# A cached-attention decode block: V as the moving operand, wo in three parts, c and x as rows

## The chip, the core and the metric

The kernel runs on one core of a Trainium2 chip. Such a core has five engines that run side by side[...]: TensorE (PE, matrix products, whose weight loads are shown as PEld), VectorE (DVE), ScalarE (ACT), GpSimd (POOL) and SyncE (SP, which here only issues transfers). Sixteen DMA engines move data between memory (HBM) and the on-chip buffer (SBUF); matrix products land in a small accumulator memory (PSUM). The metric is the time of one execution on the device in microseconds (us). Before the change it is 360.23 us, the median of 3 runs (360.12 to 360.32).

## What is computed

One token goes through a transformer block with modulation (adaLN): a modulation vector from `c`, a layer norm, attention over a cache of 32768 positions with 32 query heads on 8 kv heads of 128, an output projection, and a ReLU feed-forward of 1792. Everything is bf16 in memory.

```python
mod = (_silu(c) @ w_mod).reshape(c.shape[0], 6, 1, -1)
sa, ca, ga, sb, cb, gb = (mod[:, i] for i in range(6))
h = _layernorm(x) * (1 + ca) + sa
q = (h @ wq).reshape(B, Sq, 32, 128).transpose(0, 2, 1, 3)
scores = einsum('bhqd,bhkd->bhqk', q, repeat(k_cache, 4)) * 128 ** -0.5
o = einsum('bhqk,bhkd->bhqd', softmax(scores), repeat(v_cache, 4))
x = x + ga * (o.transpose(0, 2, 1, 3).reshape(B, Sq, 4096) @ wo)
h = _layernorm(x) * (1 + cb) + sb
x = x + gb * (maximum(h @ w1, 0) @ w2)
```

The K cache and the V cache hold 64 MB each; with the weights (w_mod 3 MB, wq 4, wo 4, w1 1.75, w2 1.75) some 149 MB have to be read for one token.

## The kernel before

**The stream.** All large inputs come through one ring of eight SBUF slots (`ring`, L71), in the order of the list `stream` (L114 to L123), by transfers that SP issues one after the other (`load`, L110). A transfer is issued when its slot is free, that is, when what was in the slot has been used. `need(key)` makes the list advance up to that key. The order is: two parts of w_mod, two of wq, four K tiles of head 0, then for each kv head g the K tiles of head g+1 and the V tiles of head g in turn; the first half of wo ahead of the last head's V tiles, then the second half of wo, w1 and three parts of w2 (1, 0.5 and 0.25 MB). A K or V tile is 2 MB: 128 partitions by 64 positions by 128. A head has four of each (NTILE = 4).

**The start.** `c` and `x` are loaded by the ACT queue with 4 elements to a partition (L134, L135), and cast (L174, L176). From c come the SiLU (L212 to L218) and 96 matmuls for the modulation (L226); `rows4` (L233) turns a column vector into four rows; `layernorm_T` (L181) does the norm with a matmul for the sums (L189); 128 matmuls give the queries (L267). POOL clears the buffers `qbd` and builds identities.

**One head.** `scores(g, u)` (L296) transposes a K tile in two halves on DVE (L309) and does 16 matmuls of 512 columns with the block-diagonal queries `qbd` as weights (L318). `softmax(g)` (L329) finds the maximum through two small matmuls (L334, L346), does the exponent on ACT (L351), transposes the probabilities on DVE (`PT_g`, L356) and gets the sums by a matmul (L361). `pv(g, u)` (L366) multiplies V: each of the 64 blocks of 128 positions is loaded as weights and met by four columns of PT_g, so that a tile costs 64 weight loads and 64 matmuls of four columns (L374), with the result transposed already. `normalise(g)` (L379) divides by the sums and spreads the result over `oA` with a mask `cmask`; `spread(b)` (L392) makes from four heads the operand `o2` for the projection; `project(b)` (L402) does 64 matmuls against half of wo (L407). The loop (L414 to L433) interleaves scores of head g+1 with pv of head g. The first half of wo is projected ahead of the last head's V tiles, the second after them.

**The tail.** With the attention summed in `attnT_ps`, DVE forms x1T (L438, L439), `layernorm_T` gives h2T, 56 matmuls the hidden vector (L450), ACT the ReLU (L455); `rows4` turns x1T into rows (L456), then 56 matmuls of 128 columns multiply by w2 (L465) as its parts land; two DVE operations (L471, L473) scale and add, and SP issues the output (L474).

[...] The transfers of the ring carry an order token, so that SP keeps their order; the rest is ordered by dependences and priorities (`tc.high_priority()` around L324).

Of the kernel before, what the change touches and what calls it, by code (L numbers as in the profile page):

```python
# [9 lines left out]
BF16 = mybir.dt.bfloat16  # L10
# [7 lines left out]
def kernel(  # L18
# [14 lines left out]
    nc = tc.nc  # L33
# [11 lines left out]
    NG = NTILE // 2  # L45
    GH = 4
    HH = GH * REP
    CH = P // HH
    RH = Dh // CH
    NHALF = Hkv // GH  # L50
    FB = 2
# [11 lines left out]
    wq_v = A_wq.rearrange("(p kt) n -> p kt n", p=P)  # L63
    wo_v = A_wo.rearrange("(b p r) d -> b p r d", p=P, r=RH)
    w1_v = B_w1.rearrange("(p kt) f -> p kt f", p=P)
# [20 lines left out]
    def load(key):  # L86
        kind = key[0]
        if kind == "wm":
            t = ring.tile([P, KT // 2, 6 * D], BF16, tag="slot", name="wm_sb")
            src = wm_v[:, 2 * key[1]:2 * key[1] + 2, :]  # L90
        elif kind == "wq":
            t = ring.tile([P, KT // 2, Hq * Dh], BF16, tag="slot", name="wq_sb")
            src = wq_v[:, 2 * key[1]:2 * key[1] + 2, :]
        elif kind == "k":
            t = ring.tile([P, TK, Dh], BF16, tag="slot", name="Ksb")
            src = kv[key[1], key[2]]
        elif kind == "v":
            t = ring.tile([P, TK, Dh], BF16, tag="slot", name="Vsb")
            src = vv[key[1], key[2]]
        elif kind == "wo":  # L100
            t = ring.tile([P, RH, D], BF16, tag="slot", name="wo_sb")
            src = wo_v[key[1]]
        elif kind == "w1":
            t = ring.tile([P, KT, Dff], BF16, tag="slot", name="w1_sb")
            src = w1_v
        else:
            a0, n = W2P[key[1]]
            t = ring.tile([P, n, FB, D], BF16, tag="slot", name="w2_sb")
            src = w2_v[:, a0:a0 + n]
        i = nc.sync.dma_start(out=t[:], in_=src)  # L110
        tc.stamp_issue_order_token(i.ins, "sp_stream")
        loaded[key] = t

    stream = [("wm", 0), ("wm", 1), ("wq", 0), ("wq", 1)]  # L114
    stream += [("k", 0, u) for u in range(NTILE)]
    for g in range(Hkv):
        if g == Hkv - 1:
            stream.append(("wo", 0))
        for u in range(NTILE):
            if g + 1 < Hkv:  # L120
                stream.append(("k", g + 1, u))
            stream.append(("v", g, u))
    stream += [("wo", 1), ("w1",)] + [("w2", i) for i in range(len(W2P))]  # L123
    pos = [0]
# [7 lines left out]

    xc_bf = const.tile([P, 2, KT], BF16)
    nc.scalar.dma_start(out=xc_bf[:, 0, :], in_=c[0].rearrange("(p kt) -> p kt", p=P))  # L134
    nc.scalar.dma_start(out=xc_bf[:, 1, :], in_=A_x[0, 0].rearrange("(p kt) -> p kt", p=P))  # L135

# [10 lines left out]
    for hp in range(4):  # L147
# [11 lines left out]

    cmask = const.tile([P, CH], F32)  # L160
    nc.vector.tensor_reduce(
        out=cmask[:], in_=ident_f[:].rearrange("p (c r) -> p c r", r=RH), op=ALU.add, axis=AX.X,
    )
    rsel_f = const.tile([P, RH], F32)
    nc.vector.tensor_reduce(
        out=rsel_f[:], in_=ident_f[:].rearrange("p (c r) -> p r c", r=RH), op=ALU.add, axis=AX.X,
    )
    rsel = const.tile([P, RH], BF16)
    nc.vector.tensor_copy(out=rsel[:], in_=rsel_f[:])
    oT_sb = const.tile([P, Hq], BF16)  # L170
    oA = [const.tile([P, HH, CH], BF16, name=f"oA{i}") for i in range(NHALF)]

    cT = const.tile([P, KT], F32)
    nc.vector.tensor_copy(out=cT[:], in_=xc_bf[:, 0, :])  # L174
    xT = const.tile([P, KT], F32)
    nc.vector.tensor_copy(out=xT[:], in_=xc_bf[:, 1, :])  # L176

# [3 lines left out]
    def layernorm_T(src_T, stat_in, dst_T, shiftT, nscaleT, tagp):  # L181
# [6 lines left out]
        stat_ps = small_ps([P, 2], f"stat_ps_{tagp}")  # L188
        nc.tensor.matmul(stat_ps[:], lhsT=onesD_f[:], rhs=stat_in[:], start=True, stop=True)  # L189
        nu = const.tile([P, KT], F32, name=f"nu_{tagp}")  # L190
# [21 lines left out]
    e_t = const.tile([P, KT], F32)  # L212
    nc.scalar.activation(out=e_t[:], in_=cT[:], func=ACT.Exp, scale=-1.0)
    nc.vector.tensor_scalar(out=e_t[:], in0=e_t[:], scalar1=1.0, scalar2=None, op0=ALU.add)
    sig = const.tile([P, KT], F32)
    nc.vector.reciprocal(out=sig[:], in_=e_t[:])
    siluT = const.tile([P, KT], BF16)
    nc.vector.tensor_tensor(out=siluT[:], in0=cT[:], in1=sig[:], op=ALU.mult)  # L218

# [12 lines left out]

    def rows4(src_T, name):  # L233

        r_ps = small_ps([P, P], f"{name}_ps")
        nc.vector.memset(r_ps[:], 0.0)
        for i in range(KT):
            dst = r_ps[32 * i:32 * i + 1, :].rearrange("o (n kt) -> o kt n", kt=KT)
            for kt in range(KT):
                nc.tensor.matmul(  # L240
                    dst[:, kt, :], lhsT=src_T[:, kt:kt + 1], rhs=ident_f[:, 32 * i:32 * i + 32],
                    start=True, stop=True, skip_group_check=True,
                )
        r_sb = const.tile([P, P], F32, name=f"{name}_sb")
        nc.vector.tensor_copy(out=r_sb[:], in_=r_ps[:])
        return r_sb

    gb_rows = rows4(modT_sb[:, 5 * KT:6 * KT], "gb_rows")

    hT = const.tile([P, KT], BF16)  # L250
    stat1 = const.tile([P, 2], F32)
    nc.vector.reduce_sum(out=stat1[:, 0:1], in_=xT[:], axis=AX.X)
    nca = const.tile([P, KT], F32)
# [6 lines left out]
    )  # L260
    layernorm_T(xT[:], stat1, hT[:], modT_sb[:, 0:KT], nca[:], "ln1")

# [103 lines left out]
    def pv(g, u):  # L366
        if u == 0:
            o_tiles[g] = ps_o.tile([P, REP], F32, tag="o", name="oT_ps")
        oT_ps, PT_g = o_tiles[g], PT_tiles[g]
        Vsb = need(("v", g, u))  # L370
        G, s0 = u // 2, 4 * (u % 2)
        for j in range(TK):
            c0 = (16 * G + j % 16) * 32 + REP * (s0 + j // 16)
            nc.tensor.matmul(  # L374
                oT_ps[:], lhsT=Vsb[:, j, :], rhs=PT_g[:, c0:c0 + REP],
                start=(u == 0 and j == 0), stop=(u == NTILE - 1 and j == TK - 1),
            )

    def normalise(g):  # L379

        b, gl = divmod(g, GH)
        o_g = oT_sb[:, REP * g:REP * (g + 1)]
        nc.vector.tensor_tensor(out=o_g, in0=o_tiles.pop(g)[:], in1=Linv_tiles.pop(g)[:], op=ALU.mult)  # L383
        nc.vector.tensor_tensor(
            out=oA[b][:, REP * gl:REP * (gl + 1), :],
            in0=o_g.unsqueeze(2).to_broadcast([P, REP, CH]),
            in1=cmask[:].unsqueeze(1).to_broadcast([P, REP, CH]), op=ALU.mult,
        )

    o2_tiles = {}  # L390

    def spread(b):  # L392

        o2_ps = small_ps([P, RH], "o2_ps")
        nc.tensor.matmul(
            o2_ps[:], lhsT=oA[b][:].rearrange("p h c -> p (h c)"), rhs=rsel[:], start=True, stop=True,
        )
        o2 = spool.tile([P, RH], BF16, tag="o2_sb", name="o2_sb")
        nc.vector.tensor_copy(out=o2[:], in_=o2_ps[:])
        o2_tiles[b] = o2  # L400

    def project(b):  # L402
        o2 = o2_tiles.pop(b)
        wo_sb = need(("wo", b))
        for r in range(RH):
            for ko in range(KT):
                nc.tensor.matmul(  # L407
                    attnT_ps[:, ko:ko + 1],
                    lhsT=wo_sb[:, r, :].rearrange("p (m ko) -> p ko m", ko=KT)[:, ko, :],
                    rhs=o2[:, r:r + 1], start=False, stop=(b == NHALF - 1 and r == RH - 1),  # L410
                    skip_group_check=True,
# [6 lines left out]
    for g in range(Hkv):  # L418
        if g + 1 < Hkv:
            build_qbd(g + 1)  # L420
        for u in range(NTILE):
            if g + 1 < Hkv:
                scores(g + 1, u)
            pv(g, u)
        PT_tiles.pop(g)
        if g + 1 < Hkv:
            softmax(g + 1)
        normalise(g)
        if g % GH == GH - 1:
            spread(g // GH)  # L430
        if g == Hkv - 2:
            project(0)
    project(1)  # L433


    stat2 = const.tile([P, 2], F32)
    x1T = const.tile([P, KT], F32)
    nc.vector.tensor_tensor(out=x1T[:], in0=attnT_ps[:], in1=modT_sb[:, 2 * KT:3 * KT], op=ALU.mult)  # L438
    nc.vector.scalar_tensor_tensor(  # L439
        out=x1T[:], in0=x1T[:], scalar=1.0, in1=xT[:], op0=ALU.mult, op1=ALU.add, accum_out=stat2[:, 0:1],  # L440
    )
    h2T = const.tile([P, KT], BF16)
    layernorm_T(x1T[:], stat2, h2T[:], modT_sb[:, 3 * KT:4 * KT], ncb[:], "ln2")

    w1_sb = need(("w1",))
# [9 lines left out]
    nc.scalar.activation(out=hidT[:], in_=hidT_ps[:], func=ACT.Relu)  # L455
    x1_rows = rows4(x1T[:], "x1_rows")  # L456
    ffn_ps = small_ps([P, P], "ffn_ps")
    nc.vector.memset(ffn_ps[:], 0.0)
    for part, (base, n) in enumerate(W2P):
# [10 lines left out]
    o_rows = const.tile([P, P], F32)  # L470
    nc.vector.tensor_tensor(out=o_rows[:], in0=ffn_ps[:], in1=gb_rows[:], op=ALU.mult)  # L471
    o_bf = const.tile([P, P], BF16)
    nc.vector.tensor_tensor(out=o_bf[:], in0=o_rows[:], in1=x1_rows[:], op=ALU.add)  # L473
    nc.sync.dma_start(  # L474
        out=out[0, 0].rearrange("(i n) -> i n", i=KT),
# [32 lines left out]
```

## Time and profile before

| | us or share |
|---|---|
| median of 3 runs | 360.23 us |
| the profiled execution's own time | 360.0 us |
| its span, first to last instruction | 358.2 us |
| PE busy (matmuls) | 237.5 us, 66% |
| PE weight loads | 136.9 us, 38% |
| DVE busy | 184.5 us, 52% |
| ACT busy | 27.0 us, 8% |
| mean granted PE clock | 0.77 |
| HBM read | 149.42 MB, 417 GB/s over the span |

The span is what the profile sees; the execution's own time is 1.8 us longer. A row of the profile names the line, the engine, the operation, the tile written and those read, and how often; busy time of an engine that waits for something else costs nothing. These groups are touched by the change (busy us and mean ns of one, then idle time before them and what ended it):

```
L318 PE MATMUL S_ps<-KTt,qbd 128*128 128x512 bf16 x512 | 159.1, 475 | 59.8 <-DVE KTt L309 58.9
L374 PE MATMUL oT_ps<-PT_g,Vsb 128*128 128x4 bf16 x2048 | 56.6, 164 | 9.5 <-DMA Vsb<-in_A_v_cache_dram 5.1
L407 PE MATMUL attnT_ps<-o_sb,wo_sb 128*128 128x1 bf16 x128 | 4.6, 172 | 2.3 <-DMA wo_sb<-in_A_wo_dram 2.3
L174 DVE CAST cT<-xc_bf 128x4 f32<-128x4 bf16 x1 | 3.8, 3764 | 4.2 <-DMA xc_bf<-in_c_dram 4.2
```

Matmuls are pipelined, so the mean of one (475 ns) is longer than the step from one to the next. The small loads of c and x land 4.4 and 8.5 us after their issue; a K or V tile lands 34 us after its issue, since it stands behind those issued before it.

### The profile page before, as it was taken

How to read it: one execution, taken by the hardware profiler on the slowest of the kernel's cores; microseconds unless marked ns; L12 is line 12 of the kernel's file. 1: busy time of each engine (PE TensorE's matmuls, PEld its weight loads, DVE VectorE, ACT ScalarE, POOL GpSimd, SP SyncE). 2: the span in 40 equal slices, each digit the busy share in tenths (PEclk: the TensorE clock that was granted, in tenths of full speed). 3: DMA queues.
4: the chain of work that ended last, by engine and by line, in shares of the span. 5: the costliest groups of instructions: out<-in, count | busy, mean ns of one | idle time of the engine just before them, and what ended most of it. 6: DMA issues, size and time to landing. Idle time of an engine off the chain costs nothing.

```text
span 358.2 us, 6817 instructions
## 1 busy us (share of the span) xinstructions
PE 237.5 (66%) x3138; PEld 136.9 (38%) x3138; DVE 184.5 (52%) x207; ACT 27.0 (8%) x65; POOL 8.3 (2%) x13
## 2 busy tenths in 40 slices
PE   0547775857587839755777758883956576895454
PEld 0543333433254425423343425341523334445354
DVE  4419976552954465553954385456655394342012
ACT  1111022002000110002000200011000100003000
POOL 9000000000000000000000000000000000000000
PEclk9999996986597659876698659686968869665555
DMA  7999999999999999999999999999999999999993
GB/s 302 428 434 423 430 437 432 417 435 432 434 421 437 428 426 432 434 424 432 434 429 424 432 429 435 426 426 432 428 435 427 423 435 434 426 426 435 426 413 119
DMA packets 11492, 149.86 MB, mean 418 GB/s; under 512 B 1480, under 2 KB 1480, under 8 KB 2376
## 3 DMA queue, kind: packets, MB, share of 16 engines
q1 hardware_dynamic: 11176, 149.43, 98.0%
q8 instruction: 24, 0.39, 0.4%
q10 hardware_dynamic: 288, 0.00, 0.0%
q14 instruction: 4, 0.03, 0.0%
HBM read 149.42 MB, written 0.00 MB: 417 GB/s over the span
## 4 chain that ended last, share of the span: by engine, by line
DMA 77%; DVE 11%; PE 10%; issue 1%; ACT 0%; DVEq 0%
DMA Ksb<-in_A_k_cache_dram 67%; DVE KTt L309 9%; DMA wo_sb<-in_A_wo_dram 9%; PE S_ps L318 6%; PE oT_ps L374 1%; DMA xc_bf<-in_c_dram 1%; PE attnT_ps L407 1%; PE ffn_ps L465 0%; PE hidT_ps L450 0%; ACT P_g L351 0%; DVE PT_g L356 0%; PE x_rows_ps L240 0%; DVE S_g L324 0%; PE stat_ps_ln L189 0%; PE L_ps L361 0%
## 5 line engine op out<-in xcount | busy, mean ns | idle before, releaser
L318 PE MATMUL S_ps<-KTt,qbd 128*128 128x512 bf16 x512 | 159.1, 475 | 59.8 <-DVE KTt L309 58.9
L309 DVE STREAM_TRANSPOSE KTt<-Ksb 128x2048 f32<-128x2048 f32 x64 | 143.7, 2286 | 47.6 <-DMA Ksb<-in_A_k_cache_dram 47.6
L318 PEld LDWEIGHTS <-qbd 128*128 128x128 bf16 x512 | 59.3, 117 | 148.5 <-issue 117.8
L374 PE MATMUL oT_ps<-PT_g,Vsb 128*128 128x4 bf16 x2048 | 56.6, 164 | 9.5 <-DMA Vsb<-in_A_v_cache_dram 5.1
L374 PEld LDWEIGHTS <-Vsb 128*128 128x128 bf16 x2048 | 56.3, 97 | 16.8 <-DMA Vsb<-in_A_v_cache_dram 5.4
L324 DVE TENSOR_SCALAR_CACHE_REDUCE S_g<-S_ps 128x512 f32<-128x512 f32 x16 | 11.0, 687 | 50.8 <-PE S_ps L318 50.8
L289 ACT COPY qbd<-qrep_sb 32x128 bf16<-32x128 bf16 x32 | 9.4, 295 | 187.0 <-PE S_ps L318 185.8
L356 DVE STREAM_TRANSPOSE PT_g<-P_g 128x1024 bf16<-128x1024 bf16 x8 | 10.0, 1245 | 17.5 <-ACT P_g L351 17.5
L361 PE MATMUL L_ps<-Lexp,ones_f 128*128 128x4 f32 x16 | 4.5, 351 | 21.1 <-DVE Lexp L359 21.1
L361 PEld LDWEIGHTS L_ps<-Lexp,ones_f 128*128 128x128 f32 x16 | 4.0, 311 | 21.5 <-issue 21.5
L383 DVE TENSOR_TENSOR oT_sb<-oT_ps,Linv 128x4 bf16<-128x4 f32 x8 | 1.3, 162 | 20.4 <-PE oT_ps L374 20.4
L226 PE MATMUL modT_ps<-siluT,wm_sb 128*128 128x1 bf16 x96 | 3.5, 172 | 10.8 <-DVE siluT L218 10.6
L351 ACT ACTIVATE P_g<-S_g,nbias 128x1024 bf16<-128x1024 f32 x8 | 9.2, 1147 | 0.2
L348 ACT ACTIVATE nbias<-Mb_ps 128x1 f32<-128x1 f32 x8 | 1.4, 172 | 90.2 <-PE Mb_ps L346 90.2
L226 PEld LDWEIGHTS <-wm_sb 128*128 128x128 bf16 x96 | 3.4, 118 | 10.8 <-DMA wm_sb<-in_w_mod_dram 7.5
L267 PE MATMUL qT_ps<-hT,wq_sb 128*128 128x1 bf16 x128 | 3.7, 165 | 5.2 <-DVE hT L207 2.7
L346 PE MATMUL Mb_ps<-ident_f,Mexp 1*128 1x1 f32 x16 | 3.5, 284 | 5.5 <-DVE Mexp L341 5.5
L407 PE MATMUL attnT_ps<-o_sb,wo_sb 128*128 128x1 bf16 x128 | 4.6, 172 | 2.3 <-DMA wo_sb<-in_A_wo_dram 2.3
L174 DVE CAST cT<-xc_bf 128x4 f32<-128x4 bf16 x1 | 3.8, 3764 | 4.2 <-DMA xc_bf<-in_c_dram 4.2
L346 PEld LDWEIGHTS Mb_ps<-ident_f,Mexp 1*128 1x128 f32 x16 | 2.8, 217 | 7.4 <-DVE Mexp L341 7.0
L267 PEld LDWEIGHTS <-wq_sb 128*128 128x128 bf16 x128 | 3.6, 104 | 5.3 <-issue 2.8
L407 PEld LDWEIGHTS <-wo_sb 128*128 128x128 bf16 x128 | 4.6, 119 | 2.4 <-DMA wo_sb<-in_A_wo_dram 2.4
(83 smaller groups left out, 53.5 us busy)
## 6 DMA issues: line engine op xcount, KB each, us to landing
Ksb<-in_A_k_cache_dram SPq DMA_DIRECT2D x32, 2048.0 KB, 34.0
Vsb<-in_A_v_cache_dram SPq DMA_DIRECT2D x32, 2048.0 KB, 34.5
wq_sb<-in_A_wq_dram SPq DMA_DIRECT2D x2, 2048.0 KB, 19.6
wo_sb<-in_A_wo_dram SPq DMA_DIRECT2D x2, 2048.0 KB, 31.9
wm_sb<-in_w_mod_dram SPq DMA_DIRECT2D x2, 1536.0 KB, 8.1
w_sb<-in_B_w_dram SPq DMA_DIRECT2D x1, 1792.0 KB, 33.8
w_sb<-in_B_w_dram SPq DMA_DIRECT2D x1, 1024.0 KB, 30.4
w_sb<-in_B_w_dram SPq DMA_DIRECT2D x1, 512.0 KB, 24.6
```

Of the source, the lines that this page charges most:

```text
L226: nc.tensor.matmul(modT_ps[:, j * KT + ko:j * KT + ko + 1], lhsT=lhsT[:, ko, :], rhs=siluT[:, kt:kt + 1], start=(kt == 0), stop=(kt == KT ...
L267: nc.tensor.matmul(qT_ps[:, hq:hq + 1], lhsT=wq_sb[kt // 2][:, kt % 2, hq * Dh:(hq + 1) * Dh], rhs=hT[:, kt:kt + 1], start=(kt == 0), stop ...
L289: nc.scalar.copy(out=o, in_=i)
L309: nc.vector.transpose(out=KTt[:].bitcast(F32), in_=Ksb[:, 32 * half:32 * half + 32, :].rearrange("p j d -> p (j d)").bitcast(F32),)
L318: nc.tensor.matmul(S_ps[:], lhsT=qbd[g % 2][:, hp, s, :], rhs=KTv[:, 16 * sl:16 * sl + 16, h, :, par], start=(t4 == 0 and sl == 0 and hp = ...
L324: nc.vector.tensor_scalar(out=S_tiles[g][:, G, :], in0=S_ps[:], scalar1=1.0, scalar2=None, op0=ALU.mult, op1=ALU.max, accum_out=m_tiles[g] ...
L346: nc.tensor.matmul(Mb_ps[:], lhsT=Mexp[:], rhs=ident_f[0:1, 0:1], start=True, stop=True)
L351: nc.scalar.activation(out=P_g[:], in_=S_g[:].rearrange("p g f -> p (g f)"), func=ACT.Exp, bias=nbias[:], scale=scale, accum_out=l_g[:],)
L356: nc.vector.transpose(out=PT_g[:], in_=P_g[:])
L361: nc.tensor.matmul(L_ps[:], lhsT=ones_f[:], rhs=Lexp[:], start=True, stop=True)
L374: nc.tensor.matmul(oT_ps[:], lhsT=Vsb[:, j, :], rhs=PT_g[:, c0:c0 + REP], start=(u == 0 and j == 0), stop=(u == NTILE - 1 and j == TK - 1),)
L407: nc.tensor.matmul(attnT_ps[:, ko:ko + 1], lhsT=wo_sb[:, r, :].rearrange("p (m ko) -> p ko m", ko=KT)[:, ko, :], rhs=o2[:, r:r + 1], start ...
```

## The change

- **V moves.** For kv heads 0 to 6, `pv` takes 16 columns of PT_g as weights (four blocks of positions by four query heads) and lets 512 columns of V pass: 16 weight loads and 16 matmuls to a tile, into a PSUM tile `o_ps` of 16 x 512, of which the four diagonal blocks of 4 x 128 are wanted. `normalise` copies it to SBUF on ACT (`X`) and picks and sums the diagonal blocks by four fp32 matmuls with a selection matrix `osel`. The last head, 7, keeps the old form.
- **wo in three parts.** Heads 0 to 3 (2 MB), 4 and 5 (1 MB), 6 and 7 (1 MB). In the stream the first two stand just ahead of the last V tile and the third just behind it; `project` of the first two runs ahead of the last `pv`.
- **c and x** come as rows of one partition, on SP, between the two parts of w_mod; eight small matmuls turn them into columns.
- **Residual rows.** `rows4` for x1T stands ahead of the w1 matmuls, its matmuls carry an order token `pe_tail` with the norm's, its copy is done by ACT; its PSUM tile and that of the w2 product come from the scores' pool and are cleared early.
- **The output** is issued by ACT instead of SP.

```diff
-    for g in range(Hkv):
-        if g == Hkv - 1:
-            stream.append(("wo", 0))
+    for g in range(LAST):
         for u in range(NTILE):
-            if g + 1 < Hkv:
-                stream.append(("k", g + 1, u))
-            stream.append(("v", g, u))
-    stream += [("wo", 1), ("w1",)] + [("w2", i) for i in range(len(W2P))]
+            stream += [("k", g + 1, u), ("v", g, u)]
+    stream += [("v", LAST, u) for u in range(NTILE - 1)]
+    stream += [("wo", 0), ("wo", 1), ("v", LAST, NTILE - 1), ("wo", 2)]
+    stream += [("w1",)] + [("w2", i) for i in range(len(W2P))]
...
-    xc_bf = const.tile([P, 2, KT], BF16)
-    nc.scalar.dma_start(out=xc_bf[:, 0, :], in_=c[0].rearrange("(p kt) -> p kt", p=P))
-    nc.scalar.dma_start(out=xc_bf[:, 1, :], in_=A_x[0, 0].rearrange("(p kt) -> p kt", p=P))
+    need(("wm", 0))
+    xc_row = const.tile([1, 2, D], BF16)
+    stream_dma(xc_row[:, 0, :], c)
+    stream_dma(xc_row[:, 1, :], A_x[0])
+    need(("wm", 1))
...
+        if u == 0:
+            o_tiles[g] = ps_o.tile([16, 4 * Dh], F32, tag="o", name="o_ps")
+        for j in range(16):
+            c0 = (16 * G + j) * 32 + REP * s0
             nc.tensor.matmul(
-                oT_ps[:], lhsT=Vsb[:, j, :], rhs=PT_g[:, c0:c0 + REP],
-                start=(u == 0 and j == 0), stop=(u == NTILE - 1 and j == TK - 1),
+                o_tiles[g][:], lhsT=PT_g[:, c0:c0 + 16],
+                rhs=Vsb[:].rearrange("p (s j) d -> p s j d", j=16)[:, :, j, :],
+                start=(u == 0 and j == 0), stop=(u == NTILE - 1 and j == 15),
             )
...
+        if g != LAST:
+            X = spool.tile([16, 4 * Dh], F32, tag="X", name="X")
+            nc.scalar.copy(out=X[:], in_=oT_ps[:])
+            oT_ps = ps_o.tile([P, REP], F32, tag="oT", name="oT_ps", bufs=1)
+            for s in range(4):
+                nc.tensor.matmul(
+                    oT_ps[:], lhsT=X[:, s * Dh:(s + 1) * Dh], rhs=osel[:, s, :], start=(s == 0), stop=(s == 3),
+                )
...
+            if g == LAST and u == NTILE - 1:
+                for i in range(len(WOP) - 1):
+                    project(i)
             pv(g, u)
...
-        if g == Hkv - 2:
-            project(0)
-    project(1)
+    project(len(WOP) - 1)
...
-    nc.sync.dma_start(
+    nc.scalar.dma_start(
         out=out[0, 0].rearrange("(i n) -> i n", i=KT),
```

## Prediction

> **What bounds the kernel now.** I read the page from the top: the slices first, then the DMA queues, then the tail in the timeline.
>
> ```profile
> DMA  7999999999999999999999999999999999999993
> GB/s 302 428 434 423 430 437 432 417 435 432 434 421 437 428 426 432 434 424 432 434 429 424 432 429 435 426 426 432 428 435 427 423 435 434 426 426 435 426 413 119
> ...
> q1 hardware_dynamic: 11176, 149.43, 98.0%
> q8 instruction: 24, 0.39, 0.4%
> q10 hardware_dynamic: 288, 0.00, 0.0%
> ```
>
> The DMA engines are full in all slices but the first and the last, at about 430 GB/s, while PE is busy 66% and DVE 52%. The bytes don't change, so no work saved on PE or DVE inside the stream can shorten it. The chain of waits says the same: DMA is 77% of it. Each 2 MB tile takes 4.86 us, and the list of DMA issues shows 34 us from issue to landing: seven tiles are always queued, so a consumer that is some us late starves nothing. What can move is the start, the rate, and how the stream ends. The end in windows of 1 us (last two columns: DMA share, GB/s):
>
> ```profile
> 348.00:349.00 1.00, 0.34 (x4) 0.29 (x2) 0.57 (x6) 0.00 (x0) 0.00 (x0) 0.50 1.00 406
> 349.00:350.00 1.00, 0.30 (x2) 0.21 (x1) 0.51 (x3) 0.22 (x1) 0.00 (x0) 0.50 0.87 340
> 350.00:351.00 1.00, 0.42 (x16) 0.52 (x17) 0.55 (x3) 0.07 (x1) 0.00 (x0) 0.50 0.63 246
> 351.00:352.00 1.00, 1.00 (x44) 1.00 (x42) 0.00 (x0) 0.00 (x0) 0.00 (x0) 0.50 0.54 209
> 352.00:353.00 1.00, 1.00 (x44) 0.98 (x42) 0.17 (x1) 0.18 (x1) 0.00 (x0) 0.50 0.56 211
> 353.00:354.00 1.00, 1.00 (x48) 1.00 (x43) 0.29 (x1) 0.00 (x0) 0.00 (x0) 0.50 0.42 160
> 354.00:355.00 1.00, 0.86 (x26) 0.39 (x17) 0.09 (x1) 0.00 (x0) 0.00 (x0) 0.50 0.01 2
> ```
>
> Half of the 16 engines are done at about 350 us; the other half runs on to 354.0. Every transfer here is spread evenly over all 16, so half of them lost about 4.1 us on the way. The DMA packet records of the trace say to what: queue q8, PE's instruction fetches, 24 packets of 16 KB. Take the one at 132.45 us: it holds its engine for 0.93 us, and the stream packet behind it takes 1.11 us instead of 0.61, so that engine is **1.41 us** late from there on. Followed by their landings, the same eight engines are hit in turn: 24 / 8 = 3 fetches, 3 x 1.41 = 4.2 us. That is the gap between the halves.
>
> Then the tail:
>
> ```profile
> 353.07 1.78 PE L465 MATMUL ffn_ps<-w_sb,hidT 128*1 128x128 bf16 x50
> 353.34 0.29 DVE L245 COPY x_rows_sb<-x_rows_ps 128x128 f32<-128x128 f32 x1 [0.64 <-PE x_rows_ps L240]
> 354.48 0.10 PEld L465 LDWEIGHTS <-hidT 128*1 128x1 bf16 x7 [0.19 <-issue]
> 354.91 0.29 DVE L471 TENSOR_TENSOR o_rows<-ffn_ps,gb_rows_sb 128x128 f32<-128x128 f32 x1 [1.28 <-PE ffn_ps L465]
> 355.24 0.29 DVE L473 TENSOR_TENSOR o_bf<-o_rows,x_rows_sb 128x128 bf16<-128x128 f32 x1
> 355.56 0.66 SPq L474 DMA_DIRECT2D out_dram<-o_bf  x1
> ```
>
> The last w2 part is issued at 330.87 and lands 23.6 us later, at 354.47; PE's weight loads stop for 0.19 us and resume at 354.48. So the last landing ends the stream, with PE only 0.2 us ahead of it. From there 3.7 us remain: eight matmuls, two DVE operations, the output DMA, the close.
>
> **The change, part by part.**
>
> *V moving (kv heads 0 to 6).* A V tile was 64 weight loads and 64 matmuls; it becomes 16 and 16. The compiled PE stream falls from 6,090 rows to 3,427. A fp32 row is several instructions (the rows for L361 show 16 matmuls for 8), so I count about 6,250 and 3,670: 2,580 fewer[...]. 24 fetches become 14, of which some 12 or 13 fall inside the stream. Over eight engines the worst has 2 instead of 3: the stream ends **1.41 us earlier**. With an uneven turn the worst stays at 3 (gain 0); with one round, 2.8. I take 1.41, since 9 to 16 fetches all give 2.
> [...] The q8 row (0.4% of 16 engines' span is 22.9 us, 0.95 us per fetch) and the late half of the engines say 1.41. I go by the row.
>
> *The price on PE.*
>
> ```profile
> 93.84 5.62 PE S_ps L318 x16
> 99.46 1.58 PE oT_ps L374 x64
> 101.03 3.51 PE S_ps L318 x16
> ```
>
> In the chain of waits, 64 thin matmuls take 1.58 us, and 16 of 512 columns 3.51 us at full clock, up to 6.47 at half. [...] By the average of the S_ps row (159.1 / 512 = 311 ns) it is 139 - 49.5 = 90 us and PE at 91%. Is it hidden? Per head, 38.9 us of stream, PE needs 128 x 0.219 = 28.0 us, plus the softmax turn. In that turn the new ACT copy X stands before Mb's input on ACT (estimate 0.7 us, from the 0.69 us DVE row of 512 columns; 0.4 to 1.2) and four fp32 matmuls on PE (1.1 us, twice the L361 pair; 0.6 to 2.2). DVE's oT_sb waits for them, and behind it stand KTt, PT_g, Lexp and KTt again (2.29 + 1.25 + 0.19 + 2.29 us): PE idles some 5 us. A cold clock after it adds 2.1 to 3 us (5.62 against 3.51 for one or two tiles). Sum 37 to 38 us: under 38.9, by little. About 5 us of delay in all is free at the end: V tile 7,3 lands near 342; what precedes it is done by 339 (L ends at 327.0 now, 2 us later with V tile 6,3 and X; three V tiles 5.5 us, wo0 and wo1 3.4, with waits for their landings). Cost 0.
>
> *wo in three parts, wo0 and wo1 ahead of the last V tile.* Same bytes. The 96 early matmuls (3.4 us at 36 ns) lie in the wait for the last V tile. Behind it now stand 32 instead of 64 (-1.15 us of PE) and a 1 MB landing. *Early residual rows:* 0.93 us of x_rows matmuls leave the stretch between hidT and ffn for the layernorm gap; ACT takes the copy, before hidT's Relu but long before w1 lands. *ffn_ps memset* moves up. These free PE by 2 us in the tail, but PE was only level with the last landing, and that landing still ends it: worth 0, but needed, since without them a stream that ends 1.4 us earlier would find PE 1.2 us late.
>
> *c and x as rows on SP's ring.* The ACT queue's 8-byte packets (q10, some 18 per engine at 9 ns) go: -0.15 us of every engine's time. Two short issues on SP (0.4 us each, as ACT's rows) stand ahead of wm1, covered by wm0's 3.7 us of transfer. c arrives behind wm0, at about 6.8 us instead of 5.1, but x no longer at 9.6; eight tiny matmuls follow. The wm slots free at about the same 14.5 us, with six tiles queued. Cost 0; range -0.4 to +0.1.
>
> *Output DMA from ACT instead of SP.* The ACT issues took 0.40 and 0.46 us, SP's 0.66; from issue to first packet ACT's c took 1.0 us, the output 1.27. Take -0.2 (0 to -0.3).
>
> **Sum.** -1.41 - 0.15 - 0.2 = -1.76 us: span 358.2 to 356.4; the profiled execution's own 360.0 to 358.2; against the median 360.23, **358.5 us**.
>
> **Rivals.**
> 1. *The fetch gain isn't had* (the late half has another cause, or the worst engine still gets three). Then only start and output count: 359.9. For it: nothing else ties q8 to those engines but the landings; against: size and count fit.
> 2. *More is had*: one fetch or less per worst engine before the end, and a cleaner start: -2.8 - 0.4 - 0.3 gives 356.7. Against: 12 fetches can't be one round of eight.
> 3. *PE becomes the bound*, the other side. The place is the softmax turn and the clock behind it. With 6.7 us of turn, a head fits while the mean granted clock in its 128 matmuls stays over 28 / (39.6 - 6.7) = 0.85. At 0.80 a head takes 41.7 us, 2.8 too long, six or seven times, less 5 us free: +13 us, about 372. For it: the page's mean clock is 0.77, and stretches behind a softmax sit at 0.5. Against: the low clock follows idle PE, and busy stretches are at 1.0 four us on; denser matmuls should raise it. A milder form (one us a head) just eats the gain: 360.
>
> **How the numbers follow.** Forecast 0.72 (its own range 357.9 to 359.3); rival 1 0.10; rival 2 0.07; rival 3 0.11, some 0.02 of it mild. A difference under 0.2% (0.7 us: 359.5 to 360.95) can't be told from no change. Faster: forecast and rival 2 and the lower edge of rival 1, 0.82; same 0.09; slower 0.09. The range reaches from rival 2's upper half to rival 1: 357.0 to 360.0.
>
> **What would show it.** Right: q8 with about 14 packets; full DMA share to 350 us and the half-rate stretch shorter by about 1.4 us, with the last landing near 352.8; granted clock near 1 in mid-head; PE around 80% busy; PE waiting for w2 at the end. Wrong: DMA share below 9 inside the stream, or issues to landing well under 34 us (rival 3); a half-rate stretch still four us long with 14 fetches (rival 1).

## The result, and the profile after

The changed kernel takes **358.60 us** (median of 4 runs, 358.56 to 358.75); the kernel before, beside it, 360.18 us (4 runs, 360.06 to 360.32). The ratio is 0.9957, 95% interval 0.994 to 0.9974: 1.6 us faster. The profiled execution took 358.56 us, its span is 356.8 us, the mean granted PE clock 0.90.

The page of the kernel after, first the busy times and the slices (a digit is a tenth of a slice of 8.9 us), then the DMA queues (packets, MB, share of 16 engines' span):

```profile
PE 277.3 (78%) x1859; PEld 128.6 (36%) x1859; DVE 188.0 (53%) x209; ACT 31.6 (9%) x74; POOL 8.3 (2%) x13
...
PEclk9999998999899889999999869998998989997555
DMA  8999999999999999999999999999999999999993
GB/s 307 433 432 426 428 433 430 428 434 430 428 435 426 432 434 428 434 430 430 431 430 432 430 429 437 424 432 435 424 434 431 426 435 430 428 432 434 422 414 138
...
q1 hardware_dynamic: 11316, 149.43, 98.3%
q8 instruction: 14, 0.23, 0.2%
...
q10 hardware_dynamic: 8, 0.00, 0.0%
```

The stream inside is what it was: full in every slice, about 430 GB/s. PE works more (66% to 78%), but the stream doesn't wait for it: a K tile lands 34.3 us after its issue (34.0 before). The mean granted clock is 0.90 instead of 0.77; it goes with V, for in a run below with all else of the change but V in the old form (e1) it is 0.78. Instruction fetches (q8) are 14 instead of 24. The end, in windows of 1 us (from, to, length; busy time of PE, its weight loads, DVE, ACT, POOL with counts; PE clock, DMA share, GB/s):

```profile
349.00:350.00 1.00, 1.00 (x44) 1.00 (x41) 0.00 (x0) 0.00 (x0) 0.00 (x0) 0.50 0.94 365
350.00:351.00 1.00, 0.22 (x12) 0.21 (x11) 0.00 (x0) 0.18 (x1) 0.00 (x0) 0.50 0.61 229
351.00:352.00 1.00, 1.00 (x32) 0.81 (x32) 0.00 (x0) 0.00 (x0) 0.00 (x0) 0.50 0.38 141
352.00:353.00 1.00, 0.60 (x18) 0.40 (x16) 0.00 (x0) 0.00 (x0) 0.00 (x0) 0.50 0.13 45
353.00:354.00 1.00, 0.38 (x8) 0.10 (x7) 0.45 (x2) 0.00 (x0) 0.00 (x0) 0.50 0.00 0
```

The full share lasts to 350 us as before, and the stretch in which only a part of the DMA engines still works is over at 352.6 instead of 354.2: by the packet records the last completion of the stream (a packet of 4 bytes; q1 has 1,202 of them, which is 16 to each of the 75 large transfers and one each to c and x, and the 16 are read here as one from each engine) is at 352.55 us, before it was at 354.15. That is 1.60 us, as much as the gain of the medians (1.58); the two profiled executions differ by 1.44. The timeline of the tail (start, length, engine, line, tiles, count; in brackets the idle time before it and what ended it):

```profile
348.55 1.66 PE L503 MATMUL hidT_ps<-h2T,w_sb 128*128 128x1 bf16 x56 [0.48 <-DMA w_sb<-in_B_w_dram]
...
350.98 1.02 PE L515 MATMUL ffn_ps<-w_sb,hidT 128*1 128x128 bf16 x32 [0.78 <-DMA w_sb<-in_B_w_dram]
...
352.30 1.10 PE L515 MATMUL ffn_ps<-w_sb,hidT 128*1 128x128 bf16 x24 [0.29 <-DMA w_sb<-in_B_w_dram]
...
353.02 0.10 PEld L515 LDWEIGHTS <-hidT 128*1 128x1 bf16 x7 [0.32 <-issue]
353.45 0.29 DVE L521 TENSOR_TENSOR o_rows<-ffn_ps,gb_rows_sb 128x128 f32<-128x128 f32 x1 [5.23 <-PE ffn_ps L515]
353.85 0.29 DVE L523 TENSOR_TENSOR o_bf<-o_rows,x_rows_sb 128x128 bf16<-128x128 f32 x1
354.17 1.10 ACTq L524 DMA_DIRECT2D out_dram<-o_bf  x1
```

PE waits for w1 and for every part of w2, at the third one, as before, with its weight loads (they stop for 0.32 us and go on at 353.02): the last landing ends the work. From the last completion to the end of the span it is 4.23 us, before it was 4.07.

### The profile page after: what moved, and what is told of

The parts are those of the page before. It is cut to its first block, busy times and chain, and to the rows that moved or that the text cites. A ratio compares the mean times of both kernels' runs of the same rounds, so it can differ in the third digit from the quotient of the medians.

```text
span 356.8 us, 4268 instructions
## 1 busy us (share of the span) xinstructions
PE 277.3 (78%) x1859; PEld 128.6 (36%) x1859; DVE 188.0 (53%) x209; ACT 31.6 (9%) x74; POOL 8.3 (2%) x13
## 4 chain that ended last, share of the span: by engine, by line
DMA 83%; DVE 7%; PE 5%; issue 4%; ACT 0%; SPq 0%; DVEq 0%
DMA Ksb<-in_A_k_cache_dram 66%; DMA Vsb<-in_A_v_cache_dram 9%; DVE KTt L326 6%; DMA w_sb<-in_B_w_dram 6%; PE S_ps L335 2%; PE o_ps L404 2%; DMA wm_sb<-in_w_mod_dram 2%; PE oT_ps L394 1%; DVE PT_g L373 0%; PE oT_ps L421 0%; DVE S_g L341 0%; ACT X L418 0%; PE ffn_ps L515 0%; SPq L115 0%; DVE o_rows L521 0%
## 5 line engine op out<-in xcount | busy, mean ns | idle before, releaser
L335 PE MATMUL S_ps<-KTt,qbd 128*128 128x512 bf16 x512 | 137.4, 417 | 40.1 <-DVE KTt L326 38.9
L404 PE MATMUL o_ps<-Vsb,PT_g 128*16 128x512 bf16 x448 | 103.6, 385 | 3.3 <-DVE PT_g L373 3.3
L335 PEld LDWEIGHTS <-qbd 128*128 128x128 bf16 x512 | 52.0, 104 | 115.4 <-issue 70.5
L404 PEld LDWEIGHTS <-PT_g 128*16 128x16 bf16 x448 | 38.4, 91 | 66.5 <-issue 14.9
L394 PE MATMUL oT_ps<-PT_g,Vsb 128*128 128x4 bf16 x256 | 7.6, 166 | 8.1 <-DMA Vsb<-in_A_v_cache_dram 4.4
L418 ACT COPY X<-o_ps 16x512 f32<-16x512 f32 x7 | 4.0, 575 | 84.1 <-PE o_ps L404 84.1
L394 PEld LDWEIGHTS <-Vsb 128*128 128x128 bf16 x256 | 7.5, 105 | 8.3 <-DMA Vsb<-in_A_v_cache_dram 4.5
L421 PE MATMUL oT_ps<-osel,X 16*128 16x4 f32 x56 | 7.4, 250 | 3.2 <-ACT X L418 3.2
L421 PEld LDWEIGHTS oT_ps<-osel,X 16*128 16x128 f32 x56 | 6.7, 186 | 4.6 <-ACT X L418 4.6
L154 DVE COPY sel<-ident_bf 128x128 bf16<-128x128 bf16 x4 | 7.8, 3822 | 0.4 <-POOL ident_bf masks.py:199 0.4
## 6 DMA issues: line engine op xcount, KB each, us to landing
Ksb<-in_A_k_cache_dram SPq DMA_DIRECT2D x32, 2048.0 KB, 34.3
```

The costliest lines, as they stand in the source:

```text
L154: nc.vector.tensor_copy(out=sel[:, hp, :].rearrange("p (a c) -> p a c", a=4), in_=src)
L335: nc.tensor.matmul(S_ps[:], lhsT=qbd[g % 2][:, hp, s, :], rhs=KTv[:, 16 * sl:16 * sl + 16, h, :, par], start=(t4 == 0 and sl == 0 and hp = ...
L394: nc.tensor.matmul(o_tiles[g][:], lhsT=Vsb[:, j, :], rhs=PT_g[:, c0:c0 + REP], start=(u == 0 and j == 0), stop=(u == NTILE - 1 and j == TK ...
L404: nc.tensor.matmul(o_tiles[g][:], lhsT=PT_g[:, c0:c0 + 16], rhs=Vsb[:].rearrange("p (s j) d -> p s j d", j=16)[:, :, j, :], start=(u == 0 ...
L421: nc.tensor.matmul(oT_ps[:], lhsT=X[:, s * Dh:(s + 1) * Dh], rhs=osel[:, s, :], start=(s == 0), stop=(s == 3),)
```

## The experiments

**Theory F:** PE's instruction fetches delay the DMA engines that carry them, over eight engines in turn; the engine hit most often sets the end of the stream. **Rival V:** V as the moving operand pays in another way (fewer weight loads, PE's order, the clock). **Rival T:** the edits of the start and the tail carry the gain, or a part that the V change can't show without them.

### Which part of the change it is

`e1_still8` keeps everything of the change but computes all heads in the old form:

```diff
+    STILL = Hkv - 8
...
-        if g == LAST:
+        if g >= STILL:
...
-        if g != LAST:
+        if g < STILL:
```

(The tile oT_ps also has two buffers again, as in the kernel before.)

> The changed kernel with V stationary again for all eight heads; wo in three parts, early rows, c and x as rows and the output on ACT stay. Fetch theory: PE's rows go back to about 6,100, so 24 instruction fetches, three on each of eight DMA engines; the half-rate stretch at the end is again 4 us long and the time is 360.0 us (before, less 0.2 for the start). Rival (the tail's new order is what pays): it stays near 358.6.

Measured: 359.96 us (13 runs, 359.83 to 360.05), ratio 0.9993 (0.9984 to 1.0001). Its page shows 24 fetches again, and the last completion is at 354.03.

`e2_v_only` is the other half: the kernel before with `pv` and `normalise` of the kernel after, and nothing else of the change: the hunk of V in the diff above, with its X and osel.

> The kernel before with the moving V alone (heads 0 to 6). Fetch theory: 14 fetches, last w2 landing 1.4 us earlier. If the tail's PE work was level with that landing and stays where it is, as the prediction said, PE is 1.2 us late and the time is about 360.0. If PE's tail itself hangs on landings of wo and w1, which come earlier too, it moves along, and the time is 358.8 to 359.0.

Measured: 358.65 us (5 runs, 358.5 to 359.2), ratio 0.9962 (0.9948 to 0.9976); 14 fetches, last completion 352.64. First the projection in the kernel before:

```profile
345.75 2.29 PE L407 MATMUL attnT_ps<-o_sb,wo_sb 128*128 128x1 bf16 x64 [2.29 <-DMA wo_sb<-in_A_wo_dram]
```

Then the tail of e2, where wo is still in two parts and the x_rows matmuls stand between hidT and ffn:

```profile
344.31 2.30 PE L433 MATMUL attnT_ps<-o_sb,wo_sb 128*128 128x1 bf16 x64 [2.30 <-DMA wo_sb<-in_A_wo_dram]
...
349.14 1.63 PE L476 MATMUL hidT_ps<-h2T,w_sb 128*128 128x1 bf16 x56 [1.29 <-DVE h2T L210]
...
351.64 1.72 PE L491 MATMUL ffn_ps<-w_sb,hidT 128*1 128x128 bf16 x50
...
353.42 0.29 DVE L497 TENSOR_TENSOR o_rows<-ffn_ps,gb_rows_sb 128x128 f32<-128x128 f32 x1 [1.22 <-PE ffn_ps L491]
```

PE starts the projection when wo lands, at 344.31 instead of 345.75: the landing moved with the stream, and with it everything PE does behind it. PE now runs through w2 without a stop and is done within 0.8 us of the last completion. o_rows begins at 353.42, in the full change at 353.45.

`e3_tail_only` is the kernel before with only wo in three parts, the early residual rows and the early memsets. As a difference to the kernel after, it has e1's edit and these:

```diff
-    stream_dma(xc_row[:, 0, :], c)
-    stream_dma(xc_row[:, 1, :], A_x[0])
+    nc.scalar.dma_start(out=xc_bf[:, 0, :], in_=c[0].rearrange("(p kt) -> p kt", p=P))
+    nc.scalar.dma_start(out=xc_bf[:, 1, :], in_=A_x[0, 0].rearrange("(p kt) -> p kt", p=P))
...
-    nc.scalar.dma_start(
+    nc.sync.dma_start(
         out=out[0, 0].rearrange("(i n) -> i n", i=KT),
```

> The kernel before with wo in three parts, early residual rows and early memsets alone; V stationary for all heads, c and x on ACT, output on SP. Fetch theory: 24 fetches, the last landing ends it as before: 360.2 us, within 0.2. Rival (PE's tail was the bound): up to 1 us faster, 359.2.

Measured: 360.24 us (13 runs), ratio 1.0002 (0.9994 to 1.001); 24 fetches, last completion 354.27. Worth nothing alone, and nothing on top of e2. The two hunks of this diff were also undone one at a time, with V moving: e7 has the second alone (the output by SP), e8 the first (c and x by ACT).

> The changed kernel with the output issued by SP as before. The prediction gave ACT 0.2 us: then this is 358.8. The profile after shows an ACT issue of 1.10 us against SP's 0.66 with the first packet 1.25 and 1.27 us after the issue: then it is 358.6, or up to 0.2 faster.

> The changed kernel with c and x loaded by ACT with 8 bytes to a partition as before, and cast by DVE. The prediction gave the rows on SP 0.15 us: 358.75. By the landings of the second w_mod part (9.91 us after, 10.12 before) it is 358.8. Rival: nothing, 358.6.

Measured: 358.53 us (358.31 to 358.71, ratio 0.9956, 0.9942 to 0.9969) and 358.66 us (358.62 to 358.89, ratio 0.9962, 0.9949 to 0.9974). Neither undoing costs what can be told from the full change. Rival T falls. Only with V stationary do these two show at all: e1, which has them, is 0.28 us below e3, which has not; what it comes from was not settled.

### Whether it is the fetches, and step or proportion

The number of heads in the old form sets the number of fetches. e4, e11 and e10 keep the last four, three and two of them stationary (`STILL = Hkv - 4`, `- 3`, `- 2`).

> The changed kernel with V stationary for the last four heads instead of the last one: about 4,780 PE instructions, 18 fetches. If the end is set by the engine with the most fetches, the third round over eight engines has begun, one or two engines carry three, and the whole 1.4 us is lost again: 360.0 us, although only 4 of the 10 saved fetches have come back. If the cost is spread over the engines, it is in proportion: 1.58 x 4/10 = 0.6 us, 359.2.

> The changed kernel with the last three kv heads stationary: about 17 fetches, the 17th late in the stream or behind it. Step: 358.6 if the 17th comes after the last stream transfer of its engine, else about 359.8 with one or two engines ending at 353.8 and the others by 352.5. Proportion: 359.0 to 359.1, with all late engines moved together.

> The changed kernel with the last two kv heads stationary: 15 or 16 fetches. If the engine with the most fetches sets the end, it still has two: 358.6, last completion 352.5. If the gain is in proportion to the number of fetches (1.5 us for ten): 358.9.

And `e12_fill` separates the fetches from the form of V: V moves as in the change, but PE gets instructions that only lengthen its program.

```diff
+    def fill(n):
+        f_ps = small_ps([P, 1], "fill_ps")
+        for _ in range(n):
+            nc.tensor.matmul(f_ps[:], lhsT=ident_bf[:], rhs=ident_bf[:, 0:1], start=True, stop=True)
...
+            fill(64)        # normalise, behind osel
...
+            if u == 2 and g != LAST:
+                fill(32)
```

> The changed kernel, V moving as there, plus 96 matmuls a head for heads 0 to 6 (128x1, weights and operand the identity, result unused), 32 behind the third V tile and 64 behind osel, where PE waits for KTt: 1,344 more PE instructions, so 19 fetches instead of 14, and about 3.5 us a head of PE work in a wait of some 4 us. If the number of fetches is what the time hangs on: as with the last four heads stationary (19 fetches), 359.8, with a few engines completing at 353.6 to 353.9 and the rest by 352.5. If the gain comes from V moving itself in any other way (weight loads, PE's busy time, the order of the work): 358.6, last completion 352.5. If PE becomes the bound: over 361, with issues to landing well under 32 us.

All of them with the full change and e1; fetches are q8's packets, completions those of the stream's transfers in the packet records (a late engine has one for the last w2 part, a very late one also for the part before):

| run | V of heads | fetches | last completion, us | completions after 353.3 | median, us | ratio to before (95%) |
|---|---|---|---|---|---|---|
| change | 7 moving | 14 | 352.55 | 0 | 358.60 | 0.9957 (0.994 to 0.9974) |
| e10 | 6 moving | 16 | 352.56 | 0 | 358.50 | 0.996 (0.9947 to 0.9974) |
| e11 | 5 moving | 17 | 353.96 | 1 | 359.87 | 0.9991 (0.9983 to 0.9999) |
| e4 | 4 moving | 19, the last at 353.5 us | 353.78 | 2 | 359.83 | 0.999 (0.9983 to 0.9996) |
| e12 | 7 moving, filler | 19 | 353.66 | 3 | 359.66 | 0.9991 (0.9983 to 0.9999) |
| e1 | none moving | 24 | 354.03 | 10 | 359.96 | 0.9993 (0.9984 to 1.0001) |

Two more fetches than the change: nothing. Three more: 1.3 us, nearly the whole gain, and exactly one completion is late. The 17th fetch opens the third round over eight engines; each one after it (18, 19) makes one more engine late, but the time was lost with the first. (e4's 19th, at 353.5 us, comes too late for that: two engines are late there.) One of e11's 13 executions took 358.67 us, the time without a third round. In the profiled one the 17th fetch begins at 351.9 us, near the end of the stream, so it may miss the stream at times; that is not shown, for that execution was not profiled.

A turn over sixteen engines would step at the 17th fetch as well. The durations of the fetches in the packet records speak for eight. In the kernel before they are, in ns:

| round | 1 | 2 | 3 | 4 | 5 | 6 | 7 | 8 |
|---|---|---|---|---|---|---|---|---|
| fetches 1 to 8 | 921 | 961 | 967 | 947 | 879 | 884 | 938 | 932 |
| 9 to 16 | 921 | 962 | 960 | 949 | 881 | 879 | 936 | 933 |
| 17 to 24 | 924 | 968 | 962 | 947 | 879 | 879 | 940 | 931 |

Each column keeps its own duration within 8 ns. The other runs show the same circle of eight, entered at another place, within some 10 ns (but for the first and last fetches of a run and those beside POOL's transfers in e5 and e6). Besides, a turn over sixteen would put no two of the change's 14 fetches on one engine, while its stream falls off from 350 to 352.55 us, nearly two times 1.41.

The windows of e11 (columns as above):

```profile
350.00:351.00 1.00, 0.11 (x7) 0.11 (x8) 0.00 (x0) 0.18 (x1) 0.00 (x0) 0.50 0.59 227
351.00:352.00 1.00, 0.99 (x32) 0.80 (x32) 0.00 (x0) 0.00 (x0) 0.00 (x0) 0.50 0.59 221
352.00:353.00 1.00, 0.00 (x0) 0.00 (x0) 0.00 (x0) 0.00 (x0) 0.00 (x0) 0.50 0.12 43
353.00:354.00 1.00, 0.04 (x4) 0.04 (x7) 0.00 (x0) 0.00 (x0) 0.00 (x0) 0.50 0.06 14
354.00:355.00 1.00, 0.81 (x24) 0.46 (x23) 0.14 (x1) 0.00 (x0) 0.00 (x0) 0.50 0.00 0
```

Between 353 and 354 us the DMA share is 0.06, one engine of sixteen. Nothing computes for nearly two microseconds until it is done; then PE does its 24 matmuls.

The page of e12 excludes rival V (busy times, a q8 row, the filler's group):

```profile
PE 292.3 (82%) x2531; PEld 145.3 (41%) x2531; DVE 187.6 (52%) x209; ACT 31.6 (9%) x74; POOL 8.3 (2%) x13
...
q8 instruction: 19, 0.31, 0.3%
...
L413 PE MATMUL fill_ps<-ident_bf 128*128 128x1 bf16 x672 | 19.5, 164 | 0.0
```

V moves here as in the change, PE has more to do, the DMA slices stay full, and a K tile still lands 32.9 us after its issue (34.3 in the change), so PE is not the bound. Yet 1.1 of the 1.6 us are gone, with three engines' completions late. It is the number of instructions that the time hangs on, not how V is multiplied.

### Trying to level the engines

If half of the engines end some 2.6 us after the others (350 to 352.55 us), data could be taken from the late half. e5 and e6 bring the middle part of w2 (0.5 MB) early by POOL, in 16 transfers of 8 partitions with a tiny one behind (e5) or ahead (e6) of each. The hope was that this turns the data to one half of the engines in e5 and to the other in e6; the traces don't say which engines took them.

```diff
-    stream += [("w1",)] + [("w2", i) for i in range(len(W2P))]
+    stream += [("w1",), ("w2", 0), ("w2", 2)]
...
+    for k in range(16):
+        nc.gpsimd.dma_start(out=w2b[8*k:8*k+8], in_=w2_v[8*k:8*k+8, W2P[1][0]:W2P[1][0]+W2P[1][1]])
+        nc.gpsimd.dma_start(out=pad[:, k, :], in_=A_wo[8*k:8*k+8, 0:16])
```

> The changed kernel, with the 0.5 MB middle part of w2 taken out of the stream and loaded early by POOL in 16 transfers of 8 partitions,[...] a tiny transfer of 32 bytes to a partition stands after each, so that, if the engines are taken in turn, the w2 bytes all go to one half of the engines and the tiny ones to the other. If the end is set by eight engines that carry the instruction fetches and these are one of the two halves, then w2 on the other half takes 32 KB (1.2 us) from each late engine: 357.4 us in this kernel or in the next one, and 1.2 us more (359.8) in the other of the two. If the fetching engines lie across both halves, both are 358.6 to 359.8. If the imbalance has no part in it, both stay at 358.6.

> As the one before, with the tiny transfer ahead of each w2 transfer instead of behind it, so that the halves are exchanged: 357.4 us if that one is 359.8, and 359.8 if that one is 357.4.

Measured: 364.75 us (ratio 1.013, 1.0116 to 1.0143) and 364.99 us (1.0135, 1.0121 to 1.0149). Both misses, in the same direction. The page of e5, POOL's slices, the rate and the new queue:

```profile
POOL 9644400000000000000000000000000000000000
...
GB/s 312 398 371 373 371 385 427 432 432 430 428 426 432 434 430 430 430 434 430 432 433 428 432 427 432 432 428 432 432 428 432 433 430 430 432 432 428 423 421 109
...
q0 software_dynamic: 1024, 0.53, 0.5%
```

In the five slices from 9 to 54 us the rate is 380 GB/s on the mean instead of 430: 45.4 us x (1 - 380/430) = 5.3 us of the 6.2 lost. POOL issues from 8.8 to 46.6 us, and its packets run until 55.4. They are 0.5% of the engines' time; what grew are the stream's own 16 KB packets, from 612 ns to 696 ns on the mean between 10 and 50 us in the packet records. Why they grew is not shown. At the end the DMA share falls over three us in both (from 355 to 358 us it is 0.69, 0.44, 0.26 in e5 and 0.66, 0.46, 0.15 in e6), so the pair does not tell which engines the fetches use.

`e9_w2_low8` has SP issue the same part in 16 transfers of 8 partitions:

```diff
-        stream_dma(t[:], src)
+        if key == ("w2", 1):
+            for k in range(16):
+                stream_dma(t[8 * k:8 * k + 8], src[8 * k:8 * k + 8])
+        else:
+            stream_dma(t[:], src)
```

> The changed kernel; the middle w2 part (0.5 MB) is issued by SP as 16 transfers of 8 partitions instead of one of 128. [...] If the eight engines that PE's instruction fetches delay are the other eight, the 0.5 MB are taken from the late ones (1.17 us each) and given to the early ones (+1.17 us): half-rate stretch shorter, last stream completion 351.4 instead of 352.55, time 357.4. [...] If they are mixed over both: also about 353.7, with completions in four groups. If such a transfer is spread over all engines anyway: 358.6.

That a transfer of 8 partitions runs on eight engines, the same eight each time, was assumed: "the other eight" are those that it would leave alone, and with the fetches on the eight that it takes the last completion was expected at 353.7 and the time at 359.8. The trace agrees in part: q1 has 1,314 packets of 4 bytes instead of the 1,202 of the change, 112 more, which is 16 x 8 less the 16 of the one large transfer. So each small transfer has eight completions, which fits eight engines; which eight, and whether they are always the same, it doesn't show.

Measured: 362.64 us, ratio 1.0074 (1.0061 to 1.0086), outside all that was expected. The timeline of e9:

```profile
348.93 6.01 SPq L119 DMA_DIRECT2D w_sb<-in_B_w_dram  x11
...
351.52 1.02 PE L519 MATMUL ffn_ps<-w_sb,hidT 128*1 128x128 bf16 x32 [0.90 <-DMA w_sb<-in_B_w_dram]
...
356.16 0.60 PE L519 MATMUL ffn_ps<-w_sb,hidT 128*1 128x128 bf16 x16 [3.62 <-DMA w_sb<-in_B_w_dram]
```

SP issued the last eleven of its transfers between 348.9 and 354.9; in the change the last issue begins at 332.5. The queue ran dry, at a DMA share of 0.10 from 351 to 352 us, and PE waited 3.62 us. Why SP issued them so late is not shown. Which eight engines carry the fetches stays open, and so does whether the halves can be levelled. No version here beats the change by more than can be measured.

## Why the prediction was right

- **The fetch term** (-1.41 us, 24 fetches to 14) carried the result. Its signs were full share to 350 us, a half-rate stretch shorter by about 1.4, the last landing near 352.8 and about 14 packets on q8. They came as 350, 1.6 (by completions), 353.0 (the last part is issued at 332.5 us and lands 20.5 later) and 14. All 14 begin inside the stream (the last at 350.8 us), not 12 or 13, which leaves the rounds as they were. That 9 to 16 fetches all give two rounds was forecast from the turn of eight alone; e10 (16) and e11 (17) fall on the two sides of it. The count of 14 is in proportion to the instructions that were counted, 24 x 3,670 / 6,250 = 14.1; the engine's delay gave 1.41 us, and the runs on the two sides of the step are 1.1 to 1.5 us apart.
- **The price on PE** was hidden, as forecast: PE 78% (about 80%), mean granted clock 0.90 over the whole span, where 0.85 in a head's matmuls was needed. X takes 575 ns (estimate 0.7 us), osel 7.4 / 7 = 1.06 us a head (1.1), a V tile 3.62 us (3.51). A V tile in the timeline:

```profile
135.24 3.62 PE L404 MATMUL o_ps<-Vsb,PT_g 128*16 128x512 bf16 x16
```

  The groups of the page after:

```profile
L335 PE MATMUL S_ps<-KTt,qbd 128*128 128x512 bf16 x512 | 137.4, 417 | 40.1 <-DVE KTt L326 38.9
L404 PE MATMUL o_ps<-Vsb,PT_g 128*16 128x512 bf16 x448 | 103.6, 385 | 3.3 <-DVE PT_g L373 3.3
...
L418 ACT COPY X<-o_ps 16x512 f32<-16x512 f32 x7 | 4.0, 575 | 84.1 <-PE o_ps L404 84.1
...
L421 PE MATMUL oT_ps<-osel,X 16*128 16x4 f32 x56 | 7.4, 250 | 3.2 <-ACT X L418 3.2
```

  PE's busy time rose by 39.8 us (237.5 to 277.3), and its idle time ahead of S_ps, behind KTt, fell from 59.8 to 40.1: half of the rise came out of that one wait. The scores themselves became cheaper (475 to 417 ns), with the mean clock at 0.90 instead of 0.77. In the kernel before the clock is 0.50 from 88 to 92 us, with PE busy for 0.56 us of the four, 0.76 from 96 to 100 and 1.00 from 100 to 104, with PE busy throughout; so fewer waits went with a higher clock, as forecast. By the chain of waits of before a V tile was to cost 3.51 - 1.58 = 1.93 us more, 54 us for 28 tiles, and that was right about the tile: 3.62 us against 1.58, or 226 ns a matmul. The cost was real, but it was paid out of idle time.
- **The output from ACT** (-0.2 us) was wrong: 0. By the packet records the first output packet comes 1.25 us after ACT's issue begins and came 1.27 us after SP's. The prediction took ACT's issues for c and x, 0.40 and 0.46 us, for the price; this one takes 1.10 us.
- **c and x as rows** (-0.15 us) was not seen: e8 without it is 0.06 us slower than the change, within the scatter. The early part of the stream did gain: the second w_mod part's completions moved from 10.12-10.64 to 9.91-10.38 us. Where these 0.2 us go by the end was not settled.
- **"Needed, since without them a stream that ends 1.4 us earlier would find PE 1.2 us late"** was wrong. e2 has none of the tail edits and is as fast. The step overlooked that PE's tail itself begins with landings of the same stream (wo, then w1), which come earlier by the same amount.
- The sum was -1.76, measured -1.6: the fetch term was 0.1 to 0.2 too small, the two small terms 0.35 too large together. So the mechanism was right, but that the sum came this near is in part luck: the errors cancel. In the profiled pair the last landing moved by 1.5 us (354.47 to 353.0). Why the medians moved by 1.5 to 1.6 (e2 alone: 360.19 to 358.65) and not by 1.41 stays open.

## What to carry to other kernels

Where a kernel keeps all DMA engines full, count its instructions. Here 1,344 more on PE were five more fetches (e12), and PE's matmuls and weight loads are some 265 to a fetch (6,276 with 24 before, 3,718 with 14 after); a fetch put its DMA engine 1.41 us behind. What counted is the engine that is hit most often, so a cut in instructions paid in steps (17 fetches 359.87 us, 16 fetches 358.50), and one that didn't cross a step paid nothing (16 fetches 358.50, 14 fetches 358.60). Before calling an edit necessary, ask whether the work that it moves starts at a landing that the main change moves too.

## What the runs showed of the hardware

- PE's instruction fetches (queue q8: 14 packets in the change, 19 with 1,344 more PE instructions in e12) go to eight DMA engines in turn, as far as traces without engine names can show it: their durations come back after every eighth (879 to 968 ns, each within 8 ns of its like), and completions after 353.3 us number 0, 0, 1, 2, 3 with 14, 16, 17, 18 and 19 fetches inside the stream.
- With small transfers issued by POOL beside the full stream, the stream's own packets were longer: 16 KB in 696 ns on the mean instead of 612 (e5, 10 to 50 us).
- With 16 small transfers in SP's queue behind large ones, the last part of w2 was issued at 354.6 us (e9), without them at 332.5 (the change).
- An estimate from these: the K and V passes alone need 64 tiles of 32 PE instructions with both moving, 2,048 (16 matmuls and 16 weight loads to a tile, as the page after has them), or 7.7 fetches at 265 each, ahead of all else that PE does. So a single round over the eight engines seems out of reach for this form of kernel; it was not tried.
